# Merged score phases, fused sink scores and a new plan for a windowed-attention and SwiGLU kernel

## The chip, the cores and the metric

One core of one Trainium2 chip. The metric is device time of one execution in microseconds (us); a time below is the median of several executions. A ratio is the mean time of one kernel's fast runs over the mean of the other's fast runs of the same rounds, so it is not quite the ratio of the medians beside it. "Same" means within 2%. "The head" is the first 25 us. Engines: PE is TensorE (PEld its weight loads), DVE VectorE, ACT ScalarE, POOL GpSimd, SP SyncE.

## The reference, cut to what matters

```python
# q, k, v: (4 sequences, 8 heads, 768 tokens, 64), float32
scores = q @ k.transpose(0, 1, 3, 2) / sqrt(64)
keep = (key < 4) | ((row - key >= 0) & (row - key < 128))   # 4 sink tokens, window of 128
a = softmax(where(keep, scores, -1e9))
x = (a @ v)                       # -> (3072 tokens, 512)
xn = x / sqrt(mean(x * x) + 1e-6) * rms_g
g = xn @ w_gate                   # 512 -> 1536
out = (g * sigmoid(g) * (xn @ w_val)) @ w_out
```

The 768 tokens of a sequence are six blocks of 128, so there are 24 blocks. A block of keys meets its own block of queries and the next one; the last block of a sequence meets only its own. The sink tokens reach later query blocks through a separate small product, the sink scores.

## The kernel before

A small planner in the program simulates the engines, the load queue and the eight PSUM banks, takes at each step the operation that can start first, and emits the engines' instructions in that order. A wrong duration in the planner therefore makes no wrong result, only an order with waits in it.

```python
    F32_LOADS = ("ks0","qs0")     # k and q of block 0: float32 on SP's queue, cast on chip
    GROW = "SP"                   # the row of norm gains, also on SP
    LOADS = "q-1 k-1 v-0 w-0-2 v-1 qkv-2 qkv-3 w-2-4 w-4-6 w-6-8 w-8-9 w-9-12 qkv-4 ..."
    PE_MASKS = 2                  # blocks whose mask is a matmul into PSUM before the scores
    WARM = 30
    SPLIT = (0,1)                 # blocks whose scores come in two parts
    CHUNKS = (4,2,2)
    GB_PRIO = 2000
...
    def warm(i):
        ps = bank(("warm",)) if i == 0 else BANK[("warm",)]
        nc.tensor.matmul(out=ps[:, 0:P], lhsT=zeros, rhs=zeros, start=True, stop=True)
...
    def unit_gb():                # gain row to all partitions: float32 matmul with K = 1
        nc.tensor.matmul(out=bank(("gb",)), lhsT=ones, rhs=grow, start=True, stop=True)
...
    def scores(g, n0, n1):        # 64-row tiles, two heads at a time
        b, t = divmod(g, NT)
        qkT = T["qkT", b]
        for u in range(2):
            for j in range(2):
                hp = 2 * u + j
                for hi in range(2):
                    pr = slice(hi * D, (hi + 1) * D)
                    slot = ("s", g, u, hi)
                    if slot not in BANK:
                        bank(slot)
                    nc.tensor.matmul(
                        out=BANK[slot][:, j * 256 + n0 * P:j * 256 + n1 * P],
                        lhsT=qkT[pr, 1, hp, t * P:(t + 1) * P],
                        rhs=qkT[pr, 0, hp, (t + n0) * P:(t + n1) * P],
                        start=g >= PE_MASKS, stop=True, skip_group_check=True,
                    )
...
    def sink_s(b, t, n):          # 32-column tiles, four at a time
        ps = bank(("ss", b, t))
        for hp in range(HP):
            nc.tensor.matmul(
                out=ps[hp * SW:(hp + 1) * SW, 0:n * P],
                lhsT=T["ksk", b][:, hp * SW:(hp + 1) * SW],
                rhs=T["qkT", b][:, 0, hp, t * P:(t + n) * P],
                start=True, stop=True, tile_position=(0, hp * SW), skip_group_check=True,
            )
...
        for n0, n1 in parts:      # for each block g: one score phase (or two), planned by itself
            needs = [("kT", g)] + [("qT", g + i) for i in range(n0, n1)] + gate_of(g)
            pe(220 * (n1 - n0), lambda g=g, n=(n0, n1): scores(g, *n), needs,
               [("s", g, n0)] + ([("s", g)] if last else []), pa + 1 + n0,
               takes=slots if g >= PE_MASKS and n0 == 0 else (), mode=1)
...
            for t0, n in ((2, 2), (4, 2)) if b < 2 else ((2, 4),):   # sink phases, also alone
                pe(n * 53 + 16, lambda b=b, t0=t0, n=n: sink_s(b, t0, n),
                   [("ksk", b), ("s", g + 1)] + [("qT", g + t0 + i) for i in range(n)],
                   [("ss", b, t0)], -1000.0 + 10 * (g + t0) + 2, takes=[("ss", b, t0)], mode=3)
```

The softmax here doesn't subtract the row's maximum and nothing guards it: scores larger than these inputs give would overflow.

## Time and profile before

| | before |
|---|---|
| time, median of 3 | 246.67 us (246.51 to 246.71) |
| span of the profiled execution | 244.3 us |
| PE busy | 232.6 us, 95% |
| idle PE before 25 us | 6.2 us |
| changes of PE tiling in program order | 60 |

The stretches cut at 25 and 56 us (columns as in the prediction's second fence):

```profile
0.00:25.00 25.00, 18.83 (x246) 13.78 (x247) 16.34 (x60) 15.67 (x38) 20.43 (x31) 1.00 1.61 163
25.00:56.00 31.00, 30.79 (x474) 26.00 (x476) 26.52 (x68) 20.77 (x44) 21.73 (x25) 1.00 2.01 173
56.00:241.00 185.00, 182.96 (x1384) 108.02 (x1399) 140.59 (x356) 94.75 (x195) 46.66 (x59) 1.00 0.88 95
```

Two cautions in reading them. This trace has 525, 522 and 263 records of the three feed-forward (FFN) matmuls where 528, 528 and 276 were issued. Of the 2.04 us that the last line seems to leave idle, part are missing records. And "busy" of the first line includes the warm-up matmuls and work at half clock.

### The profile page before, as it was taken

Reading aid. Unit: us, or ns where it says so; the run is one execution under the profiler, and the core shown is the slowest. Engines: PE = TensorE matmul, PEld = TensorE weight load, DVE = VectorE, ACT = ScalarE, POOL = GpSimd, SP = SyncE. Lnnn points to the kernel's source line nnn. Section 1 sums busy time; section 2 is a strip of 40 time slices with the busy share of each in tenths; the row PEclk is TensorE's granted clock in tenths of the full one; section 3 lists DMA queues with packets and bytes.
Section 4 is the critical chain, followed back from the end, with each engine's and each line's share of the span. In section 5 each row is a group of like instructions: output and inputs, shape, how many; then the busy total and the mean of one; then the engine's idle time right before and its main releaser. Section 6 shows DMA issues by size and latency. Waiting matters only on the chain.

```text
span 244.3 us, 5510 instructions
## 1 busy us (share of the span) xinstructions
PE 232.6 (95%) x2098; PEld 147.8 (61%) x2120; DVE 183.7 (75%) x482; ACT 131.2 (54%) x276; POOL 88.8 (36%) x114
## 2 busy tenths in 40 slices
PE   4978999999999999999999999999999999999994
PEld 2557996875789765688875444444545544444443
DVE  4388979979899998899888499991299992377700
ACT  3886466778675837654537555735745521333111
POOL 8995755695444749423004200302504200000000
PEclk9999999999999999999999999999999999999999
DMA  8999999999999999999944544014311013200022
GB/s 112 172 170 195 192 188 188 156 146 174 171 196 130 156 124 179 142 216 133 149 35 107 133 107 86 3 21 108 120 34 21 4 21 107 86 3 0 0 86 86
DMA packets 111979, 27.22 MB, mean 111 GB/s; under 512 B 102097, under 2 KB 109009, under 8 KB 111954
## 3 DMA queue, kind: packets, MB, share of 16 engines
q0 software_dynamic: 80704, 13.90, 81.0%
q1 hardware_dynamic: 31106, 12.85, 27.0%
q8 instruction: 16, 0.26, 0.5%
q10 hardware_dynamic: 144, 0.13, 0.2%
q14 instruction: 9, 0.07, 0.1%
HBM read 28.31 MB, written 6.29 MB: 142 GB/s over the span
## 4 chain that ended last, share of the span: by engine, by line
PE 77%; DVE 9%; POOL 5%; DMA 4%; issue 3%; ACT 0%; POOLq 0%; DVEq 0%; ACTq 0%
PE o L790 23%; PE g L757 21%; PE v L757 21%; PE s L456 4%; DMA wg<-in_moe_w_gate_dram 4%; DVE hT L780 2%; PE av L520 2%; DVE p L770 2%; PE av L515 2%; DVE r L560 2%; POOL v L327 1%; DVE xr L564 1%; PE av L505 1%; PE o_last L808 1%; DVE x L532 1%
## 5 line engine op out<-in xcount | busy, mean ns | idle before, releaser
L757 PE MATMUL g<-xnt,wg 128*128 128x128 bf16 (+2 forms) x525 | 69.8, 282 | 1.6 <-DMA wg<-in_moe_w_gate_dram 1.2
L757 PE MATMUL v<-xnt,wv 128*128 128x128 bf16 (+2 forms) x522 | 71.0, 281 | 0.3
L764 ACT ACTIVATE th<-g 128x512 bf16<-128x512 f32 x72 | 42.9, 600 | 46.7 <-PE g L757 45.2
L790 PE MATMUL o<-wo,hT 128*128 128x512 bf16 x263 | 62.6, 379 | 1.2 <-issue 0.6
L770 DVE SCALAR_TENSOR_TENSOR p<-th,g 128x512 bf16<-128x512 bf16 x72 | 48.1, 683 | 16.6 <-ACT th L764 16.2
L757 PEld LDWEIGHTS <-wg 128*128 128x128 bf16 x528 | 43.1, 98 | 21.0 <-DMA wg<-in_moe_w_gate_dram 1.5
L757 PEld LDWEIGHTS <-wv 128*128 128x128 bf16 x528 | 42.6, 98 | 18.5 <-issue 0.8
L469 ACT ACTIVATE e<-s 128x512 bf16<-128x512 f32 (+1 forms) x104 | 48.4, 542 | 6.6 <-PE s L456 6.3
L780 DVE TENSOR_TENSOR hT<-p,v 128x512 bf16<-128x512 bf16 x72 | 47.2, 682 | 1.5 <-PE v L757 0.6
L790 PEld LDWEIGHTS <-hT 128*128 128x128 bf16 x276 | 25.6, 98 | 28.7 <-issue 1.3
L491 POOL TENSOR_SCALAR_AFFINE_SELECT e<-e 128x512 bf16<-128x512 bf16 x14 | 9.4, 680 | 61.8 <-ACT e L469 48.8
L798 ACT ACTIVATE osb<-o 128x512 f32<-128x512 f32 x23 | 13.8, 599 | 29.0 <-PE o L790 29.0
L323 POOL DMA_DIRECT2D k<-in_k_dram x23 | 20.5, 890 | 15.9 <-DMA v<-in_v_dram 7.0
L323 POOL DMA_DIRECT2D q<-in_q_dram x23 | 20.5, 893 | 13.0 <-DMA k<-in_k_dram 3.8
L327 POOL DMA_DIRECT2D v<-in_v_dram x24 | 21.3, 889 | 10.0 <-DMA q<-in_q_dram 6.0
L532 DVE TENSOR_TENSOR x<-av,rden 128x256 bf16<-128x256 f32 x48 | 20.4, 425 | 1.7
L540 ACT ACTIVATE sq<-x 128x512 bf16<-128x512 bf16 x24 | 15.2, 632 | 9.4 <-DVE x L532 9.3
L531 DVE RECIPROCAL rden<-av 128x4 f32<-128x4 f32 x48 | 8.5, 177 | 15.4 <-PE av L520 15.3
L486 DVE TENSOR_TENSOR e<-e,masks 128x1024 bf16<-128x1024 bf16 (+1 forms) x30 | 18.9, 650 | 1.0 <-ACT e L469 0.8
L564 DVE SCALAR_TENSOR_TENSOR xr<-x,r,gb 128x512 bf16<-128x512 bf16 x24 | 19.0, 790 | 0.9
L520 PE MATMUL av<-v,e 128*128 128x65 bf16 x192 | 16.9, 194 | 0.0
L515 PE MATMUL av<-v,e 128*128 128x65 bf16 x160 | 15.0, 193 | 0.0
(70 smaller groups left out, 177.2 us busy)
## 6 DMA issues: line engine op xcount, KB each, us to landing
out_dram<-osb SPq DMA_DIRECT2D x23, 256.0 KB, 2.2
v<-in_v_dram POOLq DMA_DIRECT2D x24, 128.0 KB, 10.4
q<-in_q_dram POOLq DMA_DIRECT2D x23, 128.0 KB, 10.9
k<-in_k_dram POOLq DMA_DIRECT2D x23, 128.0 KB, 10.8
wo<-in_moe_w_out_dram POOLq DMA_DIRECT2D x2, 768.0 KB, 12.0
wg<-in_moe_w_gate_dram POOLq DMA_DIRECT2D x4, 256.0 KB, 7.8
wv<-in_moe_w_val_dram POOLq DMA_DIRECT2D x4, 256.0 KB, 8.2
wg<-in_moe_w_gate_dram POOLq DMA_DIRECT2D x1, 384.0 KB, 9.4
```

Of the source, the lines that this page charges most:

```text
L323: nc.gpsimd.dma_start(out=T[name, g], in_=block_of(src, g))
L327: nc.gpsimd.dma_start(out=V16[b][:, t, :, 0:D], in_=block_of(v, g))
L469: nc.scalar.activation(out=T["e", g, u][:, 2 * hi:2 * hi + 2, n0:n1, :].rearrange("p x n c -> p x (n c)"), in_=ps.rearrange("p (j c) -> p ...
L515: nc.tensor.matmul(out=dest, lhsT=T["e", g - 1, u][:, x, 1, :], rhs=V16[b][:, t - 1, h, :], start=(t == 1), stop=False, skip_group_check=True,
L520: nc.tensor.matmul(out=dest, lhsT=T["e", g, u][:, x, 0, :], rhs=V16[b][:, t, h, :], start=(t == 0), stop=True, skip_group_check=True,)
L532: nc.vector.tensor_tensor(out=T["x16", g][:, 4 * u:4 * u + 4, :], in0=pvv[:, :, 0:D], in1=rden.unsqueeze(2).to_broadcast((P, 4, D)), op=AL ...
L564: nc.vector.scalar_tensor_tensor(out=T["xr", g], in0=T.pop(("x16", g)).rearrange("p h d -> p (h d)"), scalar=r[:, 3:4], in1=gb, op0=ALU.mu ...
L757: nc.tensor.matmul(out=ps[:, i * n:(i + 1) * n], lhsT=w_sb[:, kt, ft * P:(ft + 1) * P], rhs=T["xnt", G][:, kt, cols], start=(kt == 0), sto ...
L764: nc.scalar.activation(out=T["th", key], in_=BANK[("g", key)], func=ACT.Tanh, scale=0.5,)
L770: nc.vector.scalar_tensor_tensor(out=T["p1", key], in0=T.pop(("th", key)), scalar=1.0, in1=BANK.pop(("g", key)), op0=ALU.add, op1=ALU.mult,)
L780: nc.vector.tensor_tensor(out=T[hk][:, i:i + n, cols], in0=T.pop(("p1", key)).rearrange("p (n c) -> p n c", n=n), in1=BANK.pop(("v", key)) ...
L790: nc.tensor.matmul(out=BANK[("o", G, tb)], lhsT=T["h", G, ft // 4][:, ft % 4, tb * P:(tb + 1) * P], rhs=wo[:, ft, :], start=(ft == 0), sto ...
```

## The change

Its intent: every change between 128x128 tiles and the 64-row or 32-column tiles of the scores costs PE time (about 0.1 us in the traces here), so make fewer of them. The last block of the second and of the third sequence gets its scores inside the next block's phase (two banks instead of four). From the second sequence on, sink scores run inside a score phase. The head is laid out anew: q of block 0 through ACT's queue, no warm-up matmuls, the third block masked on PE, the first FFN units two weight tiles wide, another order of the loads, and a planner with another model of the load queue, gates and margins.

```diff
-    F32_LOADS = ("ks0","qs0")
-    GROW = "SP"
+    F32_LOADS = ("ks0","qa0")
+    GROW = "ACT"
-    LOADS = "q-1 k-1 v-0 w-0-2 v-1 qkv-2 qkv-3 w-2-4 w-4-6 w-6-8 w-8-9 w-9-12 qkv-4 wo-0-6 qkv-5 wo-6-12 qkv-6 qkv-8 qkv-7"
+    LOADS = "q-1 k-1 v-0 w-4-6 qkv-2 v-1 qkv-3 w-2-4 w-6-9 w-0-1 w-1-2 w-9-10 w-10-11 qkv-4 w-11-12 wo-0-6 qkv-5 wo-6-12 qkv-8 qkv-7 qkv-6"
-    PE_MASKS = 2
+    PE_MASKS = 3
-    WARM = 30
-    GATE_LEAD = 6
-    T_LEAD = 3
-    SPLIT = (0,1)
+    WARM = 0
+    GATE_LEAD = 12
+    T_LEAD = 4
+    SPLIT = (0,)
-    GB_PRIO = 2000
+    FIRST = 2
+    SQD = 2
+    GB_PRIO = -970
+    FUSE_FROM = 1
+    MERGE = (1,2)
...
+    def scores_last(g):
+        for hi in range(2):
+            bank(("s", g, hi))
+        for hp in range(HP):
+            for hi in range(2):
+                pr = slice(hi * D, (hi + 1) * D)
+                nc.tensor.matmul(
+                    out=BANK["s", g, hi][:, hp * P:(hp + 1) * P], lhsT=qkT[pr, 1, hp, cols],
+                    rhs=qkT[pr, 0, hp, cols], start=True, stop=True, skip_group_check=True,
+                )
...
+            if merged and n0 == 0:
+                more, banks, given, other = merged
+                needs, gives, takes = needs + more, gives + given, takes + banks
+                work.insert(0, lambda g=other: scores_last(g))
+            if last and b >= FUSE_FROM:
+                for t0, n in sink_parts(b):
+                    if t0 == t:
+                        needs = needs + sink_needs(b, t0, n)
+                        takes = takes + [("ss", b, t0)]
+                        work.append(lambda b=b, t0=t0, n=n: sink_s(b, t0, n))
... (cut: the planner's new load model, margins and bank reserve; exponentials and masks of
... the last blocks; the mean square of two blocks on DVE; FFN units of variable width)
```

Counted in the order of PE's program, the tiling changes fall from 60 to 50.

## The prediction

> **What bounds the kernel now.** I read the page first (which engine fills the span), then the busy time of each engine by stretch (where that engine is not filled), then its waits, then the head of the run instruction by instruction. The page:
>
> ```profile
> span 244.3 us, 5510 instructions
> PE 232.6 (95%) x2098; PEld 147.8 (61%) x2120; DVE 183.7 (75%) x482; ACT 131.2 (54%) x276; POOL 88.8 (36%) x114
> PEclk9999999999999999999999999999999999999999
> ```
>
> TensorE (PE) is the bound: 232.6 of 244.3 us, so 11.7 us idle. The stretches say where they are:
>
> ```profile
> core 0: us, PE busy (x) PEld busy (x) DVE busy (x) ACT busy (x) POOL busy (x), PEclk, DMA share, GB/s
> 0.00:8.36 8.36, 4.68 (x29) 3.10 (x29) 3.15 (x17) 3.29 (x5) 7.15 (x14) 1.00 1.21 128
> 8.36:18.10 9.74, 8.44 (x118) 5.34 (x117) 7.11 (x26) 8.26 (x26) 9.47 (x13) 1.00 2.04 171
> 18.10:25.00 6.90, 5.71 (x105) 5.34 (x103) 6.08 (x17) 4.12 (x10) 3.81 (x6) 1.00 1.48 193
> 25.00:60.00 35.00, 34.79 (x506) 28.16 (x508) 30.38 (x80) 23.99 (x51) 23.48 (x27) 1.00 2.00 174
> 60.00:130.00 70.00, 69.52 (x695) 52.88 (x698) 63.45 (x169) 41.78 (x89) 28.93 (x33) 1.00 1.85 145
> 130.00:210.00 80.00, 78.73 (x508) 38.01 (x518) 57.71 (x152) 40.05 (x84) 15.98 (x24) 1.00 0.27 67
> ```
>
> Busy subtracted from length: 3.68 + 1.30 + 1.19 = 6.2 us idle before 25 us; 0.21 + 0.48 + 1.27 = 2.0 us from 25 to 210 us. Another 3.4 us is the tail after the last matmul (240.9 us on the chain that ended last), which the diff leaves alone. Of the middle, only this is a wait that the profile names:
>
> ```profile
> PE o L790 <- issue: 0.6, 4, 0.2
> PE g L757 <- DVE rden L531: 0.3, 1, 0.3
> ```
>
> So after 25 us there is at most about 1 us of waiting to win; the rest is PE work. Two things are hidden in "busy". First, the head runs at half speed: until 8.36 us consecutive 128-column matmuls start 106 ns apart, afterwards 56 ns; I read that from the start times, for the page's clock row shows 9 throughout. Second, 30 warm-up matmuls (line 391) count as busy and compute nothing.
>
> The head, from the order in time (SP queue, then ACT, then PE):
>
> ```profile
> 0.81 0.46 SPq L315 DMA_DIRECT2D stage<-in_k_dram  x1
> 1.33 0.46 SPq L341 DMA_DIRECT2D grow<-in_moe_rms_g_dram  x1
> 1.84 0.40 SPq L315 DMA_DIRECT2D stage<-in_q_dram  x1
> ...
> 6.33 0.62 ACT L319 CAST q<-stage 128x512 bf16<-128x512 f32 x1 [1.71 <-DMA stage<-in_q_dram]
> ...
> 4.16 1.87 PE L438 MATMUL s<-bias,idnos 128*128 128x512 bf16 x4 [2.07 <-DVE bias L273]
> 18.14 0.61 PE L757 MATMUL g<-xnt,wg 128*128 128x128 bf16 x8
> 19.75 0.62 PE L757 MATMUL g<-xnt,wg 128*128 128x128 bf16 x8 [1.00 <-DMA wg<-in_moe_w_gate_dram]
> ```
>
> The first q block, third in one queue, is there at 6.3 us, and the first scores run at 8.46. The first feed-forward (FFN) matmul runs at 18.14 although its two weight tiles landed at 9.6 and 11.0 us: a unit takes four tiles of 128 columns at once, and the second pair lands at 19.7.
>
> **What the Trainium skill says.** (1) "TensorEngine Tiling (Array Packing)", Key Properties: changing the tiling mode, not just the tile, drains TensorE. Scores use 64x128 tiles, sink scores 128x32, all else 128x128. The trace agrees and prices it:
>
> ```profile
> 37.69 0.89 PE v L757 x16
> 52.72 0.89 PE g L757 x16
> 53.61 0.54 PE s L456 x8
> 54.15 1.00 PE v L757 x16
> ```
>
> On the chain that ended last, 16 FFN matmuls of 128 columns take 0.89 us, but 1.00 after a score phase; eight scores of 256 columns, two at a time, would take 4 x 0.109 = 0.44 us (0.87 us per eight FFN matmuls of 256) and take 0.54. So 0.10 us in, 0.11 out. (2) "TensorE: Matmul & The Clock Gate", Part 1: the clock doubles after a free-running window of about 3.4 us of activity. The 106 to 56 ns step agrees in kind. (3) "DMA: Bandwidth & Descriptors", Issuing engines are not separate DMA queues: issuing from two engines saves only the issue time. Here an issue on SP takes about 0.5 us.
>
> **The change part by part.**
>
> *Switches.* In order of time I count 26 score phases and 6 sink-score phases, three of the latter directly after a score phase. After: the second block is no longer split (-1), last blocks of the second and third sequence ride in the next phase (-2): 23. 3 x 0.21 = 0.63 us. Four of six sink phases (sequences 1 to 3) are fused; one of those already stood behind a score phase and one directly before one, so about two transitions go: 0.2 us. A fused sink still changes to 128x32 tiles, so it is not free. Sum -0.8 us, all on PE and so on the path. The last blocks' eight matmuls of 128 columns stay; in two banks instead of four they need two exponentials of 128x512 (608 ns) instead of four of 128x256 (395 ns): 0.36 us of ACT per sequence, at 54% use worth nothing in itself.
>
> *Head, first scores.* q moves to ACT's queue behind the small row, so it issues about 0.5 us earlier and meets fewer of the Pool queue's loads; I estimate landing at 5.0 to 5.3 instead of 6.3. The bias is made before the second Pool load is issued: that issue took 0.91 us, so the masks start near 3.3 instead of 4.16. First scores about 1.2 us earlier. PE is still cold there, so I credit 1.0.
>
> *Head, FFN.* The first chunk's units become two tiles wide, with a weight pair loaded in the same place as now; the FFN can start once the first x is transposed (15.5 us now, 14 after the shift), not at 18.1. Squares of the first two blocks go to DVE: ACT's 0.63 + 0.19 replaced by one DVE operation, estimated at the 0.75 of the similar 128x512 step, so only a hop. Of the 2.5 us idle between 8.36 and 25 us plus about 1.2 us of warm-up matmuls (22 x 56 ns) that fill holes there, I take back 1.5: later weight pairs land no earlier than before, and the bytes ahead of them are the same.
>
> *Masks.* The third block is masked on PE: +4 x 0.216 = 0.86 us, and 2 x 0.69 = 1.4 us less DVE in its busiest early stretch. Since some of it fills idle time, I count +0.5.
>
> *Gates, orders, constants.* New leads and margins act on the 0.9 us of named waits after 25 us: -0.2.
>
> Sum: -0.8 - 1.0 - 1.5 + 0.5 - 0.2 = -3.0 us, so 243.7 us.
>
> **Rivals.**
>
> *Banks or transposes make a new wait.* A merged phase takes 2 + 4 banks, with a sink 7 of 8, at once; before it PE may only fill what is left. Emptying a g/v pair takes tanh 0.60, then 0.68 and 0.68 us on DVE. Also the fused phase of a third block in sequences 2 and 3 needs q of the sixth block, whose DMA transpose lands 7 to 8.5 us after issue in the trace, while score phases stand 6.5 to 12 us apart. For it: DVE is 63.45 of 70 us busy from 60 to 130. Against: the plan orders around both, and the transposes' lead grows from 3 to 4 blocks. If it holds, 0.5 to 2 us per place: 245 to 247.
>
> *The head is bound by bytes.* DMA is busy at 9 tenths from the second slice; FFN units that start early then wait for the next weights, and the order 4-6, 2-4, 6-9, 0-1 gives the second block's four-wide units no complete set until about 25 us. For it: the 1.00 us wait at 19.75. Against: attention of blocks 2 and 3 can fill the hole. If it holds, only switches and 1 us of head remain: 245.
>
> *Without warm-up matmuls the clock stays low one window longer.* About 3.4 us at half speed costs up to 1.7 us: 245.4. Against: masks of three blocks and transposes give PE work from 3.3 us on.
>
> *The head is emptied well.* Most of the 6.2 us idle and the warm-up goes: 240.5 to 241.5. Against: loads and DVE chains (a block's norm is some 1.8 us of small serial steps) take their time in any order.
>
> **Range and chances.** The switches (0.8) are nearly sure; the head decides, from about 0 to 5 us. 243.7, range 240.8 to 246.4. Two per cent faster is 241.7, which needs the last rival: 0.20. Slower by 2% (251.6) would take several new stalls where PE now waits 0.9 us in 216: 0.02. Within: 0.78.
>
> **What would show it.** First scores near 7.2 us, first FFN matmul near 14, PE idle before 25 us at 4 us or less; 23 score phases, each still 0.10 in and 0.11 out; PE waits after 25 us still under 1.5 us. The prediction is wrong if q lands as late as now, if the step from 106 to 56 ns comes near 12 us, if g waits for weight DMA by several us near 15 to 25, or if new PE waits on DVE, ACT or a transposed qkT stand before merged phases.

## The result, and the profile after

| | before | after |
|---|---|---|
| median of 4 runs each, same chip | 246.69 us (246.51 to 246.79) | 246.66 us (246.25 to 246.83) |
| ratio | | 0.9997, 95% interval 0.998 to 1.0014 |
| span of the profiled execution | 244.3 us (a run of 245.98) | 245.0 us (a run of 246.70) |

Nothing came of it, where 3 us were forecast. The profiled execution of before was 0.7 us faster than its median, so the two traces differ by 0.7 us where the medians do not. What has to be explained is the missing 3 us, not these 0.7.

The same three stretches of the changed kernel:

```profile
0.00:25.00 25.00, 18.60 (x202) 12.01 (x203) 14.27 (x58) 14.96 (x32) 19.67 (x30) 1.00 1.58 161
25.00:56.00 31.00, 29.57 (x462) 24.73 (x459) 25.60 (x69) 19.93 (x43) 23.34 (x28) 1.00 2.16 168
56.00:241.00 185.00, 185.00 (x1427) 109.42 (x1424) 140.57 (x354) 95.42 (x192) 52.79 (x70) 1.00 0.88 96
```

After 56 us the profile shows PE busy throughout. Before 56 us it is not: 6.4 us of idle up to 25, 1.4 from 25 to 56. All named waits of PE lie there:

```profile
PE s L481 <- DVE bias L315: 3.9, 1, 3.9
PE q L459 <- DMA q<-in_q_dram: 2.4, 2, 1.8
PE k L459 <- DMA k<-in_k_dram: 0.8, 2, 0.4
PE x L682 <- DVE xr L667: 0.5, 1, 0.5
PE g L926 <- DVE x L612: 0.2, 1, 0.2
```

The head in order of time; first ACT's queue and ACT, then PE:

```profile
1.38 0.41 ACTq L357 DMA_DIRECT2D stage<-in_q_dram  x1
...
5.48 0.62 ACT L361 CAST q<-stage 128x512 bf16<-128x512 f32 x1 [0.69 <-DMA stage<-in_q_dram]
```

```profile
6.09 2.07 PE L442 MATMUL gb<-grow,ones 1*128 1x512 f32 x2
8.09 1.03 PE L459 MATMUL q<-ident,q 128*128 128x128 bf16 x8
...
9.48 1.04 PE L499 MATMUL s<-qkT 64*128 64x128 bf16 x16
...
13.81 0.40 PE L459 MATMUL k<-ident,k 128*128 128x128 bf16 x4 [0.44 <-DMA k<-in_k_dram]
...
16.59 0.40 PE L459 MATMUL q<-ident,q 128*128 128x128 bf16 x4 [1.84 <-DMA q<-in_q_dram]
...
19.49 1.06 PE L926 MATMUL g<-xnt,wg 128*128 128x128 bf16 x16
...
26.40 0.40 PE L682 MATMUL x<-ident,xr 128*128 128x128 bf16 x4 [0.52 <-DVE xr L667]
...
31.83 0.40 PE L459 MATMUL q<-ident,q 128*128 128x128 bf16 x4 [0.56 <-DMA q<-in_q_dram]
```

q did come early: its cast starts at 5.48 instead of 6.33 us. But PE, free at 6.09, took the gain matmul, and that holds it for 2.0 us; the diff had moved it there (GB_PRIO from 2000 to -970). In the kernel before it stood after the first scores, at full clock:

```profile
8.46 0.40 PE L456 MATMUL s<-qkT 64*128 64x128 bf16 x8
8.79 1.12 PE L399 MATMUL gb<-grow,ones 1*128 1x512 f32 x2
```

The Trainium skill, "FP8 and Floating Point Precision", TensorE Precision Notes, says that true FP32 takes four passes through the array. The trace agrees: 2.00 us from start to start at half clock, against 0.53 for the same shape in one bf16 pass, measured below. So the first scores start 1.0 us later than before (9.48 against 8.46), and after two waits for queued loads the first FFN matmul is 1.35 us later (19.49 against 18.14). On the way, x of block 0 is normalised 1.7 us later (DVE ends xr at 16.10 against 14.41), and PE, whose order puts the transposes of q of block 3 and the third mask first, transposes it at 17.68 us, against 14.47 before. The clock, read from the starts and the trace's clock record, doubles at 11.6 us and not at 8.4.

**Accounts at 56 us.** I summed PE's useful work: each matmul at the distance between starts that its kind shows where nothing interrupts it at full clock (216 ns for 512 columns, 56 for 128, half for scores, a quarter for sink scores), masks, warm-ups and the gain matmul left out, and gaps of whole FFN matmuls counted as missing records (3.9 us of them in the trace of before, plus 0.9 where they fell together with a tiling change).

| | before | after | of the difference |
|---|---|---|---|
| useful work done by 56 us | 39.39 | 37.18 | 2.21 behind |
| of that: masks | 1.73 | 2.59 | 0.86 |
| tiling changes up to there | 20, about 2.1 us | 16, 1.67 us | about -0.4 |
| rest (waits, half clock, warm-ups) | | | about 1.75 |
| from 56 us to PE's last matmul | 184.82 | 185.56 | 0.74 longer, with 2.21 more to do |
| tiling changes there | 40, 4.12 us | 34, 3.53 us | -0.59 |
| idle there | 1.37 | 0.50 | -0.87 |

The useful work of the two stretches adds up to 218.63 us in both kernels, which checks the count. So the change wins 1.5 us after 56 us: 0.6 by fewer tiling changes, as its intent says, and 0.9 by less idle time. About 0.5 of the latter is one wait of the kernel before, for DVE at 138.4 us. The change loses 2.2 before 56 us, where a gain of 2 to 2.5 was forecast.

### The profile page after: what moved, and what is told of

Read it like the earlier page. It is cut to its first block, busy times and chain, and to the rows that moved or that the text cites. A ratio compares the mean times of both kernels' runs of the same rounds, so it can differ in the third digit from the quotient of the medians.

```text
span 245.0 us, 5460 instructions
## 1 busy us (share of the span) xinstructions
PE 233.7 (95%) x2086; PEld 146.4 (60%) x2086; DVE 180.9 (74%) x480; ACT 130.3 (53%) x266; POOL 95.8 (39%) x126
## 4 chain that ended last, share of the span: by engine, by line
PE 78%; DMA 12%; POOL 7%; issue 1%; DVE 1%; POOLq 0%
PE o L965 23%; PE v L926 23%; PE g L926 22%; DMA k<-in_k_dram 4%; DMA wo<-in_moe_w_out_dram 4%; DMA wv<-in_moe_w_val_dram 4%; PE s L499 3%; PE av L600 2%; POOL v L369 2%; POOL q L365 1%; PE av L593 1%; POOL wg L412 1%; POOL wv L412 1%; PE av L583 1%; PE o_last L983 1%
## 5 line engine op out<-in xcount | busy, mean ns | idle before, releaser
L926 PE MATMUL g<-xnt,wg 128*128 128x128 bf16 (+2 forms) x528 | 71.0, 282 | 0.2 <-DVE x L612 0.2
L937 ACT ACTIVATE th<-g 128x512 bf16<-128x512 f32 (+1 forms) x75 | 43.2, 587 | 50.7 <-PE g L926 50.2
L965 PE MATMUL o<-wo,hT 128*128 128x512 bf16 x276 | 65.3, 379 | 0.0
L944 DVE SCALAR_TENSOR_TENSOR p<-th,g 128x512 bf16<-128x512 bf16 (+1 forms) x75 | 48.3, 661 | 21.3 <-ACT th L937 21.1
L954 DVE TENSOR_TENSOR hT<-p,v 128x512 bf16<-128x512 bf16 (+1 forms) x75 | 47.7, 659 | 3.3 <-PE v L926 3.0
L547 ACT ACTIVATE e<-s 128x512 bf16<-128x512 f32 (+1 forms) x84 | 43.1, 590 | 6.0 <-PE s L499 6.0
L569 POOL TENSOR_SCALAR_AFFINE_SELECT e<-e 128x512 bf16<-128x512 bf16 x14 | 8.9, 638 | 38.4 <-ACT e L547 19.6
L667 DVE SCALAR_TENSOR_TENSOR xr<-x,r,gb 128x512 bf16<-128x512 bf16 x24 | 18.4, 766 | 0.9
L630 ACT ACTIVATE sq<-x 128x512 bf16<-128x512 bf16 x22 | 13.9, 633 | 7.3 <-DVE x L612 7.2
L600 PEld LDWEIGHTS <-e 128*128 128x128 bf16 x192 | 13.1, 97 | 2.4 <-ACT e L547 0.2
```

The costliest lines, as they stand in the source:

```text
L547: nc.scalar.activation(out=T["e", g, u][:, 2 * hi:2 * hi + 2, n0:n1, :].rearrange("p x n c -> p x (n c)"), in_=ps.rearrange("p (j c) -> p ...
L600: nc.tensor.matmul(out=dest, lhsT=own, rhs=V16[b][:, t, h, :], start=(t == 0), stop=True, skip_group_check=True,)
L667: nc.vector.scalar_tensor_tensor(out=T["xr", g], in0=T.pop(("x16", g)).rearrange("p h d -> p (h d)"), scalar=r[:, 3:4], in1=gb, op0=ALU.mu ...
L926: nc.tensor.matmul(out=ps[:, i * n:(i + 1) * n], lhsT=w_sb[:, kt, ft * P:(ft + 1) * P], rhs=T["xnt", G][:, kt, cols], start=(kt == 0), sto ...
L937: nc.scalar.activation(out=T["th", key], in_=BANK[("g", key)][:, 0:n], func=ACT.Tanh, scale=0.5,)
L944: nc.vector.scalar_tensor_tensor(out=T["p1", key], in0=T.pop(("th", key)), scalar=1.0, in1=BANK.pop(("g", key))[:, 0:n], op0=ALU.add, op1= ...
```

## The experiments

Eighteen kernels; all gave a correct result but for the three that are marked. Where "after" stands without more, the changed kernel is meant. For all runs with the changed kernel's PE order, I followed a few landmarks; the numbers are us against the changed kernel's own trace (top row: its times).

| | first scores | scores of block 1 | q of block 3 | first FFN | q of block 4 | k, 7th transpose | 7th score phase | PE's end |
|---|---|---|---|---|---|---|---|---|
| after | 9.48 | 14.14 | 16.59 | 19.49 | 31.83 | 50.14 | 55.55 | 241.56 |
| gb16 | -1.46 | -0.02 | -0.21 | +1.49 | +0.51 | -0.01 | -0.01 | -0.01 |
| spin | -1.59 | -0.09 | -0.09 | +2.26 | +1.47 | +0.96 | +0.95 | +0.95 |
| gb16_spin | -1.86 | -0.02 | -0.18 | +2.18 | +1.56 | +1.05 | +1.04 | +1.03 |
| fill | -1.96 | -0.15 | -0.16 | -0.16 | -0.75 | -0.71 | +0.54 | +0.54 |
| resplit | 0.00 | +0.34 | +0.34 | +0.34 | -0.28 | +0.24 | +0.85 | +2.03 |
| earlyq4 | 0.00 | +0.30 | -0.46 | +1.14 | +0.17 | -0.34 | -0.35 | -0.26 |
| earlyq34 | 0.00 | +0.01 | -1.89 | -0.42 | +1.43 | +0.92 | +0.91 | +1.01 |
| q4_fill | -2.00 | +0.09 | +0.16 | +0.16 | -0.55 | +0.16 | +0.59 | +0.59 |
| q3q4_fill | -2.18 | -0.16 | -1.99 | +0.34 | +1.05 | +0.53 | +0.52 | +0.52 |
| q3q4 | 0.00 | +0.46 | -1.45 | -0.33 | -0.71 | -0.21 | +0.41 | +0.41 |
| q3q4_narrow | -1.72 | +0.30 | -1.55 | -0.03 | -0.53 | -0.70 | +1.04 | +1.03 |
| light | 0.00 | +0.30 | -1.60 | -0.66 | -1.24 | -1.76 | -1.77 | -1.77 |
| fill_light | -1.76 | -0.94 | -1.27 | -1.28 | -1.94 | -2.45 | -2.46 | -2.47 |

Read the last two columns first. But for resplit, which adds work throughout, what a kernel has at 55.5 us it has at the end, to 0.1 us. So this half of the run is bound by PE alone, and everything is decided before. These are single profiled executions; the medians with intervals are given with each run.

### Are the tiling changes on the path?

**resplit** parts again what was merged: one 128x128 matmul between the two halves of a merged phase and before each fused sink, in the same order; 8 more changes, 6 more matmuls.

```diff
+    def apart(ps):
+        nc.tensor.matmul(out=ps[:, 0:P], lhsT=ident, rhs=ident, start=True, stop=True, ...)
+                work.insert(0, lambda g=g: apart(bank(("s", g, 0, 0))))
+                         work.append(lambda b=b, t0=t0: apart(bank(("ss", b, t0))))
```

> The changed kernel in its own order, with one idle 128x128 matmul (56 ns, into a bank that is overwritten next) between a phase and each of the four sinks and between the two halves of the two merged phases: the named mechanism undone without another plan. 8 more changes of tiling mode at 0.105 us and 6 x 0.056 us: 1.18 us longer than the changed kernel, 247.7 to 248.1, if the switches lie on the path. Rival: they sit where PE would wait anyway, under 0.4 us longer, below 247.2.

Measured: 248.26 us (before in the same rounds 246.5), ratio 1.0054, 1.0029 to 1.0079. From 55.5 us to the end it loses 1.18 us against after: 8 changes at 0.105 us and 6 matmuls at 56 ns make 1.18. The changes are on the path, at their full price. Ten fewer are worth about 1.05 us.

**nofuse** is the changed kernel without merging or fusing, and planned anew for it.

```diff
-    FUSE_FROM = 1
-    MERGE = (1,2)
+    FUSE_FROM = 9
+    MERGE = ()
```

> The changed kernel without its two named mechanisms (sink scores on their own, no last block shares a phase), everything else as in the change, replanned. 56 changes of tiling mode in the PE order instead of 50; at 0.105 us each 0.63 us longer: 247.1 to 247.5. Rival: the wide phases (6 or 7 banks at once) cost as much as the switches save: 246.4 to 246.9. Rival 2: they cost more, below 246.3.

Measured: 253.35 us (251.29 to 256.21) against 246.85, ratio 1.0238, 1.0208 to 1.0267: slower. With 56 changes instead of 50 it should lose some 0.6 us. It lost 6.5. In the profiled execution the new plan put PE behind a mask on POOL, and the clock fell to half at 119 to 122 us:

```profile
PE av L600 <- POOL e L569: 2.9, 2, 2.2
```

The fall of the clock is only a part: the fastest execution had a mean clock of 1.0 and still took 251.29 us. So this run says nothing on the price of the changes. It says that one replanning can move the time by more than the whole change.

### Is it PE's work in the head: the gain matmul, the clock?

**gb16** makes the gain matmul one bf16 pass (upper halves of the float32 numbers); **spin** puts 24 dummy matmuls before the masks; **gb16_spin** does both; **fill** adds dummies before the transposes that wait for loads, so that the clock stays up.

```diff
-        nc.tensor.matmul(out=bank(("gb",)), lhsT=ones, rhs=grow, start=True, stop=True)
+        nc.tensor.matmul(out=bank(("gb",)), lhsT=ones.bitcast(BF16)[:, 1::2],
+                         rhs=grow.bitcast(BF16)[:, 1::2], start=True, stop=True)
```

```diff
+        for _ in range(24 if g == 0 else 0):
+            nc.tensor.matmul(out=BANK["s", 0, 0, 0][:, 0:P], lhsT=spin, rhs=spin, start=True, stop=True)
```

```diff
+        for _ in range({('q', 2): 24, ('k', 2): 6, ('q', 3): 28}.get((n, g), 0)):
+            nc.tensor.matmul(out=ps[:, 0:P], lhsT=spin, rhs=spin, start=True, stop=True)
```

> The changed kernel in exactly its own order on every engine; only the fp32 matmul that spreads the gain row over the partitions (two passes, 2.07 us on the cold PE from 6.09 to 8.16 us in the changed kernel's trace) runs as one bf16 pass (gain truncated to bf16; a wrong rounding on purpose). Theory A (the head is a chain: what PE loses before the first scores reaches the end of the run): first scores at about 7.9 instead of 9.48 us, the run 1.0 to 1.5 us shorter, 245.2 to 245.7. Theory B (the head is held by the arrival of loads: q of block 2 was waited for 1.84 us until 16.59, q and k of block 4 later): first scores earlier all the same, the waits for q and k loads grow by as much, the run 246.4 to 246.8.

> The changed kernel in its own order, with 24 dummy matmuls of 128 columns put on PE before its first mask matmul, into the bank that the mask then overwrites. They fill 1.1 to 3.7 us, where PE waits for the bias. The clock should step up near 8.3 us instead of 11.6. Theory A: some 3 us of PE work between 8.3 and 11.6 run at full instead of half rate, the run 1.0 to 1.5 us shorter, 245.2 to 245.7. Theory B: same clock step, waits for q loads grow, 246.4 to 246.8. Theory C (the window of the clock runs freely, dummy work does not move it): step stays near 11.6, time unchanged.

> Both edits in one, own order. Theory A: gains nearly add, 244.2 to 245.2, first scores near 7.3 us. Theory B: still 246.3 to 246.8, PE waits longer for the q and k loads of blocks 2 to 4.

> gb16_spin with 24, 6 and 28 more dummy matmuls just before the transposes of q of block 2, k of block 2 and q of block 3, where PE waits for those loads; order otherwise that of the changed kernel. The clock should step up near 5 us and stay up (it fell at 12.2 us in gb16_spin). Theory B2 (the head is held by the loads of block 3, landing near 16.5 us, and the fall of the clock is what made gb16, spin and gb16_spin slower than the change): back to the time of the change, 246.3 to 246.8. Theory A: the earlier first scores are worth something once the clock stays up, 245.0 to 245.8.

| | this | before | ratio, 95% interval | granted clock full |
|---|---|---|---|---|
| gb16 | 247.51 | 246.85 | 1.0018, 1.0003 to 1.0034 | 9.8 to 13.2, again from 20.1 us |
| spin | 247.52 | 246.85 | 1.0014, 0.9994 to 1.0035 | 5.1 to 15.3, again from 22.1 |
| gb16_spin | 247.01 | 246.85 | 1.0011, 0.9995 to 1.0027 | 5.4 to 12.2, again from 22.4 |
| fill | 247.29 | 246.5 | 1.0029, 1.0014 to 1.0044 | 4.5 to the end |

All four brought the first scores forward by 1.5 to 2.0 us, which is what the prediction wanted of the head, and none ended earlier. gb16's trace shows the lead going into the waits for the next loads:

```profile
6.10 0.60 PE L442 MATMUL gb<-grow,ones 1*128 1x512 bf16 x1
...
12.60 0.40 PE L462 MATMUL q<-ident,q 128*128 128x128 bf16 x4 [1.08 <-DMA q<-in_q_dram]
...
16.37 0.60 PE L462 MATMUL q<-ident,q 128*128 128x128 bf16 x4 [1.22 <-DMA q<-in_q_dram]
```

By the scores of block 1, 0.02 us is left of 1.46. At 13.24 us the clock fell again; by the first FFN matmul the kernel was 1.5 us behind, and later waits that shrank took that back. fill settles the clock: it ran at full clock from 4.5 us on, 2 us ahead, and still had only 0.15 us left at 14 us. It got 0.75 ahead by 31 us, and lost that and more in the loads of the later blocks:

```profile
52.38 0.40 PE L471 MATMUL q<-ident,q 128*128 128x128 bf16 x4 [0.79 <-DMA q<-in_q_dram]
```

So, as long as the loads stand as they do, repairing the gain matmul and the clock brings back none of the missing 3 us.

**before_nowarm** is the kernel before with its 30 warm-up matmuls left out, the order else unchanged.

```diff
     def warm(i):
         ps = bank(("warm",)) if i == 0 else BANK[("warm",)]
-        nc.tensor.matmul(out=ps[:, 0:P], lhsT=zeros, rhs=zeros, start=True, stop=True)
+        return
```

> The kernel before in its own order with its 30 warm-up matmuls left out. If they hold the clock: the step comes 3.4 us later than 8.4 us or the clock falls again in the holes up to 20 us, and the run is 0.7 to 1.7 us longer, 247.4 to 248.4. Rival (they only fill holes): 246.5 to 246.9, or a little shorter.

Measured: 246.05 us (246.0 to 246.27) against 246.5, ratio 0.9981, 0.9966 to 0.9995: not slower, and the fastest correct kernel, if by 0.2%. Its clock doubles only at 16.2 us. It is 0.74 us behind before at 33 us, 0.59 from 53 us on and 0.09 from 145 us on: the 0.5 us that the kernel before waits at 138.4 us is gone in it. So a later head did not reach the end in that kernel either.

### Is it the plan's order of loads?

In the changed kernel's plan, q of block 2 was due at 11.5 us and landed at 12.8; q of block 3 at 15.0 and 16.5; q of block 4 at 30.5 and 31.8. **recal** tells the planner so and plans anew; the others keep PE's order and move loads forward in POOL's queue.

```diff
 recal (with the edits of gb16 and spin, and 20/6/16 dummies):
+            late = 1300 if 8500 < r["POOL"] < 17300 else 0
 earlyq4:     q, k of block 4 ahead of weight tile 10
 earlyq34:    q of block 3 ahead of v of block 2, and q, k of block 4 ahead of weight tile 9
 q3q4:        q of block 3 and v of block 1 ahead of v of block 2; q, k of block 4 as in earlyq4
 q4_fill:     fill and earlyq4
 q3q4_fill:   q3q4 with fill's edits, without the 28 dummies of block 3
 q3q4_narrow: q3q4_fill with the third block's mask 128 columns wide, not 512 (wrong result on purpose)
```

> The changed kernel planned again with one correction: loads that the plan puts between 8.5 and 17.3 us land 1.3 us later in the plan, as the trace showed (q of block 2: planned 11.5, landed 12.8; q of block 3: planned 15.0, landed 16.5); with the bf16 gain matmul, the 24 dummies at the start and 20, 6, 16 before the same transposes. PE order now has the first x transposes, the third mask and the first FFN matmuls ahead of the transposes of q of block 3. Theory D (the in-order PE stood behind q of block 3 with ready work behind it): 1 to 1.5 us shorter than fill, 244.8 to 245.6. Rival (work after 16.6 us is dense anyway, what is moved ahead leaves other holes): within 0.4 us of fill.

> The changed kernel in its own order on every compute engine; on the load queue q and k of block 4 go ahead of the two weight loads (128 columns each of gate and value, tile 10) that stood before them. In all runs with the changed kernel's order so far, whatever the head gained or lost was made even by waits for loads between 12 and 54 us (first scores 1.46 us earlier in gb16, 0.00 at 55 us). Theory B (loads pin PE up to about 54 us): q and k of block 4 land some 1.4 us earlier (30.4, 31.1 instead of 31.8, 32.5), the waits of 1.2 us before their transposes go, and 0.3 to 1.2 us of it is left at the end: 245.4 to 246.3. Rival (the moved weights are then waited for, or another load takes over): within 0.3 us of the change, 246.3 to 247.0.

> As earlyq4, but q of block 3 also goes ahead of v of blocks 2 and 1 (PE waited for it 1.84 us until 16.59), and q and k of block 4 ahead of four weight loads. Theory B: first FFN matmul near 17.8 instead of 19.5 us; the end 1 to 2 us earlier than the change, 244.7 to 245.7, unless weight tiles 6 and 7 (landing 24.3 us) pin PE again, then as earlyq4.

> The change with the load order of q3q4_fill alone: no dummies, fp32 gain matmul. If the clock matters by itself: 0.5 to 1.5 us longer than q3q4_fill with the clock stepping near 11.6 us or falling in the head, 245.6 to 246.6. If loads alone pin: same as q3q4_fill.

> fill (bf16 gain matmul, dummies at the start and in the three holes, so that the clock stays up) with the load order of earlyq4. In fill PE reached q and k of block 4 0.75 us earlier than the change and waited there; in earlyq4 that wait was gone but the clock fell from 16.1 to 19.5 us and cost 1.1 us. Theory B3 (the change loses its gain to the waits of 1.4 us between 25 and 35 us and, in part of its executions, to a fall of the clock in the head): both gone, 1.0 to 1.5 us shorter than fill and 0.6 to 1.2 shorter than the change: 245.4 to 246.1. Rival (weight tile 10, now later, is waited for): within 0.3 us of fill, 247.

> As q4_fill, but q of block 3 and v of block 1 also go ahead of v of block 2 (no bytes added before any weight); no dummies before q of block 3. Scores of block 2 start 1 to 1.8 us earlier, its x is ready when PE wants it (0.5 us waited at 26.4 in the change). Theory B3: 0.3 to 0.6 us shorter than q4_fill, 244.9 to 245.7. Rival (weight tiles 6 and 7 landing at 24.3 us pin PE): same as q4_fill.

> q3q4_fill with the mask matmuls of block 2 cut from 512 to 128 columns (4 x 0.16 = 0.64 us of PE less; block 2 is left partly unmasked, a wrong result on purpose). If the third masked block is on the path, 0.5 to 0.65 us shorter than q3q4_fill; if loads (weight tiles 6 and 7) still pin PE behind it, 0 to 0.2 us.

| | this | before | ratio, 95% interval |
|---|---|---|---|
| recal | 247.95 | 246.5 | 1.0056, 1.003 to 1.0081 |
| earlyq4 | 246.88 | 246.62 | 1.0022, 1.0002 to 1.0041 |
| earlyq34 | 247.51 | 246.62 | 1.0033, 1.0016 to 1.005 |
| q3q4 | 247.25 | 246.82 | 1.0008, 0.9981 to 1.0036 |
| q4_fill | 247.87 (247.0 to 249.5) | 246.82 | 1.0048, 1.0003 to 1.0093 |
| q3q4_fill | 247.74 | 246.82 | 1.0043, 1.0012 to 1.0073 |
| q3q4_narrow (wrong) | 247.89 | 246.82 | 1.0045, 1.0014 to 1.0076 |

None of these orders gained anything. recal, with another PE order, had its first FFN matmul at 16.20 us, 3.3 us earlier than after, and PE's last matmul 0.80 us later. The table of landmarks shows the pattern: earlyq34, q3q4 and q3q4_fill have q of block 3 by 1.5 to 2 us earlier, and are then late somewhere else. In earlyq34 the weights pushed back made PE wait 3.1 us. That is what a queue does whose bytes are all needed soon: moving one forward moves another back. q3q4_narrow takes 0.65 us of mask matmuls off PE and is no faster than q3q4_fill, so the third mask, too, costs nothing visible in this head.

One load none of these runs moved: k of block 6, in the change the last one that PE itself transposes (the eighth group of k transposes). The plan has it at 51.2 us; it landed at 53.05 in after, at 53.96 in fill and at 53.0 to 54.5 in all twelve kernels with the changed kernel's PE order and all the bytes, after included. In eight of them PE takes it within 0.15 us of its landing, in after with 0.42 us to spare. q3q4_narrow reached the seventh k transposes 0.7 us ahead, and its lead ended there: k landed at 54.45, and PE took it at 54.50, after a wait of 1.56 us. The timeline puts that wait down to DVE, but this load's own view names the weight loads of those transposes as waiting for it:

```profile
L371 POOL DMA_DIRECT2D k<-in_k_dram x1: 873/873/873, 45.0 to 45.0; - x1
...
  PEld L471: 1.7, 1
...
DMA to landing us min/median/max: 9.4/9.4/9.4
```

Had PE come more than 0.42 us earlier in after, it would have waited here. Moving this load was not tried.

### Is it the head that was given up?

**headback** is the changed kernel's planner with the head of before: its loads, queues, masks, warm-ups, gain priority and load model; merged and fused phases kept. **headback_apart** is the same without merging and fusing.

```diff
-    F32_LOADS = ("ks0","qa0")
-    GROW = "ACT"
-    PE_MASKS = 3
-    WARM = 0
-    SPLIT = (0,)
-    FIRST = 2
-    SQD = 2
-    GB_PRIO = -970
+    F32_LOADS = ("ks0","qs0")
+    GROW = "SP"
+    PE_MASKS = 2
+    WARM = 30
+    SPLIT = (0,1)
+    FIRST = 4
+    SQD = 0
+    GB_PRIO = 2000
... (also LOADS, POOL_AT, CAST_DVE and the load model of before; headback_apart: FUSE_FROM = 9, MERGE = ())
```

> The change's mechanism, gates, leads and margin with the head of the kernel before: its load order, its queues, two masked blocks, four-tile FFN units, square on ACT, 30 warm-up matmuls, and its planner's model of the loads. PE order is that of the kernel before for the first 315 matmuls, 54 changes of tiling mode. Theory: the change lost 2.2 us of PE work up to 56 us through its head and won about 1.5 us after it; with the old head only the gain is left: 244.9 to 245.9. Rival (the new plan of the middle brings its own waits, as in nofuse): 246.5 and more.

> headback without fused sinks and merged phases (60 changes of tiling mode instead of 54), planned by the same planner. If the switches are what the mechanism is worth: 0.63 us longer than headback. Rival: the plans differ by more than that through their waits, in either direction.

Measured: headback 247.18 against 246.62, ratio 1.0025, 1.0 to 1.0051; headback_apart 256.43, ratio 1.0369, 1.0306 to 1.0432, slower. Of the second, the profile shows why it is no clean comparison; it is nofuse's fault over again, with half clock from 115 to 125 us:

```profile
PE av L596 <- POOL e L565: 7.2, 2, 6.9
```

headback waits 1.0 us for that mask as well. Putting the old head before the new rest gains nothing, but since each of these is a new plan with new waits, the pair leaves open what the old head alone would be worth.

### Is it the bytes?

**light** is the changed kernel with half the weight bytes, PE's order unchanged; a wrong result. **fill_light** is fill with the same edit.

```diff
-                out=w_sb[:, :, cols], in_=src[:, :, cols]),
+                out=w_sb[:, 0:2, cols], in_=src[:, 0:2, cols]),
-        sw_load(lambda: nc.gpsimd.dma_start(out=wo[:, rows, :], in_=wo_src[:, rows, :]),
+        sw_load(lambda: nc.gpsimd.dma_start(out=wo[:, f0:(f0 + f1) // 2, :], in_=...),
-                    ... lhsT=w_sb[:, kt, ft * P:(ft + 1) * P],
+                    ... lhsT=w_sb[:, kt % 2, ft * P:(ft + 1) * P],
-                rhs=wo[:, ft, :], ...
+                rhs=wo[:, ft - 3 * (ft % 6 // 3), :], ...
```

> The changed kernel with half the weight bytes: each weight load brings two of its four row blocks (three of six for the output weights) and the matmuls read those twice. A wrong result on purpose; the order of every engine is the same. Theory (up to about 54 us the PE is pinned by the moment at which the queued loads land): all loads after the first weights land earlier, q of block 4 well before 31.78 us and k of block 6 well before 53.05, the waits for loads go, and the kernel ends 0.5 to 2.5 us below the changed kernel (244 to 246.2). Rival (the PE's own work and the PSUM hand-overs set the time; the loads are hidden): within 0.3 us of the changed kernel.

> The kernel called fill (head made 2 us earlier by a one-pass gain matmul and dummy matmuls) with the same halved weight bytes, again a wrong result on purpose. Theory (loads pin the PE): with the loads early, the lead of the head is no longer absorbed, and this ends 1 to 2.5 us below light of the same rounds, 242 to 245. Rival (the head's lead is lost to something that is not a load: clock, exponentials, PSUM): within 0.5 us of light, or above it, as fill was 0.6 us above the changed kernel.

Measured: light 244.84 us (244.52 to 244.94) against 247.05, ratio 0.9903, 0.9875 to 0.9932; fill_light 244.52 (244.21 to 244.96), ratio 0.9896, 0.9871 to 0.9922. Both wrong. PE does the same matmuls in the same order in light, only the loads arrive earlier, and 2.2 us came off (1.8 in the traces, against after). q of block 3 landed at 14.5 instead of 16.5 us, q of block 4 at 24.7 instead of 31.8, k of block 6 at 46.5 instead of 53.05, and no PE wait for a load is left in its list:

```profile
PE x L682 <- DVE xr L667: 0.9, 2, 0.7
PE q L459 <- DVE rden L611: 0.4, 1, 0.4
PE g L926 <- DVE x L612: 0.2, 1, 0.2
PE k L459 <- DVE x L612: 0.2, 1, 0.2
```

```profile
0.00:25.00 25.00, 19.79 (x214) 13.04 (x214) 14.72 (x61) 14.94 (x32) 23.80 (x36) 1.00 1.58 143
25.00:56.00 31.00, 30.28 (x474) 25.44 (x471) 26.16 (x67) 21.60 (x46) 25.25 (x30) 1.00 2.34 147
```

By 56 us light has done 39.06 us of useful work, against 37.18 of after and 39.39 of before, and keeps the lead to the end. That is within the theory's range; the rival, that loads are hidden, falls.

fill_light missed the theory's number: 0.3 us below light in the medians and 0.7 in the traces, not 1 to 2.5. By its number the rival came true (within 0.5 of light). The landmarks say where the rest went. It is 1.8 us ahead of light at the first scores and 1.2 at the scores of block 1. Its dummy matmuls, sized to bridge waits for loads that now come early, then hold PE until the q of block 3 is 0.33 us later than in light. The 0.62 to 0.70 us it has from the first FFN matmul on stay to the end (2.47 against 1.77). In fill, with all the bytes, a lead of 0.75 us at 31 us was lost by 55. So a lead is kept when the loads are early and lost when they are not; that 2 us of it would be kept, this run does not show.

## Why the prediction was wrong

**Switches, -0.8: right.** They are on the path and cost 0.105 us each; ten fewer make 1.05 us. resplit put eight changes back in and lost what they should cost. The forecast counted 23 score phases after; there are 22, since the two parts of block 0's scores now stand together.

**Head, first scores, -1.0: failed, +1.0.** "q lands at 5.0 to 5.3" was near enough (its cast starts at 5.48). The step left out what PE does when q arrives: the gain matmul, four passes at half clock, 2.0 us, started a moment before. The prediction had not asked where the new order would put it. The masks, too, started at 3.87 us and not near 3.3.

**Head, FFN, -1.5: failed, +1.35, and this is the step on which the forecast broke.** It let the FFN start once the first x is transposed, put that at 14 us, and argued that the emptied holes come back as time although "the bytes ahead of them are the same". The first x was transposed at 17.68 us, behind the wait for q of block 3, and time won in the head did not come back. PE's first 55 us are pinned at several points by loads from a busy queue; four kernels whose head was 1.5 to 2 us earlier ended level or later, seven that reordered loads or repaired the head and the loads together ended level or later, and the one edit that made all the loads earlier gained 2.2 us. The prediction named the rival "the head is bound by bytes" and gave it 245 us, because it still granted 1 us of head; in none of the runs with all the bytes was anything of the head to be had. That the bytes alone set the head is not shown: the kernel before loads the same bytes and had done 2.2 us more useful work by 56 us.

**Masks, +0.5.** The third block's masks add 0.86 us of PE work. q3q4_narrow cut them to a quarter without a gain, so beside the waits for loads they cost about nothing.

**Gates, -0.2: right in direction, too small.** Idle after 56 us went from 1.37 to 0.50 us, in one trace each. The page of the kernel before hid part of this, for its idle figures mixed waits with missing records. nofuse and headback_apart show how little this term can be known ahead: other plans of the same kind lost 6.5 and 10 us.

**The rivals.** No merged phase waits for banks or transposes: PE's list has no wait for DVE, ACT or a transposed q in the merged stretch. The half-clock rival came true as an event (the step at 11.6 us) and not as a cost: fill removed it and gained nothing, before_nowarm has it at 16.2 us and loses nothing at the end.

The sum: +1.5 us won after 56 us, by switches and plan, and lost again before, in a head that now has more work on PE and waits for the same bytes. What stays open: how much the change would win over the kernel before if both had early loads, since before was not run with halved weights; and how much of the loss before 56 us belongs to the gain matmul's place and how much to the new order of loads, because each of them alone is hidden by the other. Open, too, is what an earlier k of block 6 alone would give.

## What to carry to other kernels

Ask of a planned saving not only whether it lies on the path in its own stretch, but what the next fixed point downstream is: up to the last load that PE waits for, a lead on PE is worth only what the loads let through. Test this by changing arrival alone (half the bytes, a wrong result) before polishing what stands in front of it. And count a bound engine's work by starts, not by busy time: missing records look like waits, and warm-ups and half clock look like work.

## What the Trainium skill lacked or had wrong

- "TensorEngine Tiling (Array Packing)", Key Properties, says that changing the tiling mode drains TensorE and gives no price. Here a change costs 0.095 us into and 0.093 us out of the 64-row scores, 0.09 from these to the 32-column sink scores and 0.107 out of them; eight changes and six small matmuls cost 1.18 us in resplit. (These figures count from the last tile's start; a whole score phase pays 0.20 us for its two changes.)
- "TensorE: Matmul & The Clock Gate", HAM oscillation, states the rule of no PE-idle gaps over some 3.4 us. It is not enough (the page's next section tells of a kernel in which short idles did it, and gives no length): in gb16 the clock fell to half at 13.24 us for 6.8 us, although no wait that the profile names for PE since the clock had risen at 9.83 was over 1.1 us. In fill, with those waits filled by dummy matmuls, it stayed up. Nor does the length of a wait decide it: in after, PE waited 1.84 us up to 16.59 us and the clock stayed up.
- No page gives a test that tells a head bound by load arrival from one bound by PE; to name what each gap waits for is not that test, since a shortened wait can grow again at the next load. Here the head was 2 us shorter on PE in fill without a gain (ratio 1.0029), and half the weight bytes took off 2.2 us (ratio 0.9903).
